# LayerNorm stage of a spectral-filter and GEGLU kernel: table loaded in pieces, row sums redistributed, last tiles grouped, transform waits per row tile

## The chip, the cores and the metric

The kernel runs on one core of a Trainium2 chip. The metric is device time in microseconds (us) of one execution. TensorE is called PE, VectorE DVE, ScalarE ACT, GpSimd POOL; SP issues most of the transfers (DMA).

## The reference

```python
h  = x + irfft2(rfft2(layernorm(x)) * (w_r + 1j*w_i))        # x: 2048 x 576, bf16
h2 = h + (gelu(layernorm(h) @ w_gate) * (layernorm(h) @ w_up)) @ w_down   # 576 -> 4608 -> 576
```

## The kernel before

The transforms are matmuls with cos/sin tables. Only the first stage matters here: the LayerNorm (LN1) of 16 row tiles of x and the first matmul, over the row index. Each tile of x (128 rows x 576) needs its mean and variance. The variance becomes 1/std, and that scales not x but the tile's slice of the cos/sin table `ATB`, giving `ATS`. The row-tile matmuls multiply x by `ATS` into PSUM; the results are evicted to `U`. When `U` is complete, the transform over the other index begins (`st_D`). Its first matmul is called **D** below.

```python
for i, (c0, c1) in enumerate(((0, 2), (2, 4), (4, 8), (8, 12), (12, 16))):
    P.dma(SP, XO[:, c0:c1, 0:D], xv[:, c0:c1, :], ...)           # x in five pieces
    if i == 1:
        P.dma(SP, ATB[...], dram["ATAB"][:, :], "atb", ...)      # whole table, 512 KB, after piece 2
...
GROUPS = ((0, 2), (2, 4), (4, 8), (8, 12), (12, 14), (14, 16))
ACT_TILES = (3, 7, 11, 13)            # sums of these tiles on ACT, the others on DVE (bn_stats)

ln1_act(3)                            # ACT: sum and sum of squares of tile 3
idle_mm(18)                           # 18 filler matmuls on a zero tile, to keep PE's clock up
ln1_tile(0); ln1_tile(1); ln1_var(0); ln1_sqrt(0)      # DVE, DVE, DVE, ACT
ln1_act(7)                            # ACT: needs x piece 3
ln1_tile(2); ln1_scale(0, DVE); ln1_var(1); ln1_sqrt(1); ln1_tile(4); ln1_scale(1, POOL)
a_group(0, (ACT,) * 5)                # row-tile matmuls of group 0 and their five evictions
# ... groups 1 to 5 in the same manner (cut) ...
idle_mm(2)

def st_D(i):                          # every d-transform matmul waits for all of U
    ... P.op(PE, matmul(bank, U[:, us, g, :, :], FT[:, o, dt, :]), r=ukeys + ["FT"], ...)
```

An instruction that waits holds what is written behind it on its engine.

## Time and profile before

| | before |
|---|---|
| time, median of the first 3 runs | 508.82 us |
| span of the profiled run | 506.9 us |
| D starts | 22.47 us |
| from D to the end | 484.4 us |

The page of the kernel before: busy time and share of the span by engine, then the chain of work that ended last, by line.

```profile
PE 496.6 (98%) x4331; PEld 290.1 (57%) x4331; DVE 182.4 (36%) x376; ACT 157.6 (31%) x296; POOL 46.1 (9%) x61
...
PE PS L740 56%; PE PS L761 28%; PE PS L634 2%; PE PS L649 2%; DMA XO<-in_A_x_dram 1%; PE PS L541 1%; PE PS L579 1%; DVE T_80 L563 1%; ACT U L476 1%; DVE CUS L547 1%; PE PS L558 1%; DVE CUS L548 1%; DVE T_81 L564 1%; DVE U L474 1%; ACT JNK L411 0%
```

L740 and L761 are the feed-forward matmuls, 84% of the chain. The LN1 stage is under 5% of the span, and everything after D is fixed work, so the change is worth what D moves forward. PE's 98% says little about this stage: of the first 22 us PE counts as busy for 16.96, and some 10 of them are fillers. The Trainium skill, "Trainium Kernel Development and Optimization" (section Performance Expectations), warns that matmul busy time is a poor metric; this trace agrees, since PE looks busy while D waits for DVE and ACT.

The timeline of PE in the kernel before (start us, duration us, engine, line, operation, count, and in brackets the idle time before it and its releaser):

```profile
1.32 6.12 PE L452 MATMUL PS<-ZD 128*128 128x512 bf16 x18 [1.32 <-POOL ZD L369]
7.74 0.96 PE L463 MATMUL PS<-ATS,XO 128*128 128x128 bf16 x10 [0.30 <-DVE ATS L447]
...
11.46 0.85 PE L463 MATMUL PS<-ATS,XO 128*128 128x128 bf16 x10 [2.44 <-POOL ATS L442]
...
22.47 1.66 PE L541 MATMUL PS<-FT,U 128*128 128x290 bf16 x12 [0.35 <-DVE U L474]
```

L452 are the fillers, L463 the row-tile matmuls, L541 is D. The first row-tile matmul is at 7.74 us.

The chain of waits of the kernel before, in order of time (start us, us, what):

```profile
2.13 6.73 DMA XO<-in_A_x_dram
8.88 0.78 ACT JNK L411 x2
...
10.32 0.18 ACT RS_56 L435
10.51 1.33 ACT U L476 x5
...
20.67 1.66 DVE U L474 x5
22.33 0.14 issue
22.47 0.55 PE PS L541 x3
```

The third x piece lands at 8.86 us. ACT's sums of tile 7 (`JNK`) wait for it, and behind them stand the second group's Sqrt (`RS_56`) and all evictions (`U`). From there ACT has no pause until its last eviction, and DVE waits for ACT only twice, for 0.84 and 0.36 us. So the chain starts with a transfer, and the 512 KB table had been queued in front of that transfer.

### The profile page before, as it was taken

What the parts mean: (1) busy time and instruction counts of PE and PEld (TensorE: products, weight loads), DVE (VectorE), ACT (ScalarE), POOL (GpSimd) and SP (SyncE); (2) the same over time, 40 slices, a digit from 0 to 9 for tenths busy, and PEclk for the clock granted to TensorE, in tenths of its full rate; (3) what the DMA queues carried; (4) which work ended last, traced back from release to release, by engine and by line L of the source; (5) the groups of instructions that cost most, each with busy time, mean ns of one, the idle gap of its engine ahead of it and who ended that gap; (6) DMA issues with size and microseconds to landing.
All of it is one profiled execution on the core that took longest, in us unless ns stands there. A gap on an engine that the chain in (4) does not pass through costs nothing.

```text
span 506.9 us, 9999 instructions
## 1 busy us (share of the span) xinstructions
PE 496.6 (98%) x4331; PEld 290.1 (57%) x4331; DVE 182.4 (36%) x376; ACT 157.6 (31%) x296; POOL 46.1 (9%) x61
## 2 busy tenths in 40 slices
PE   6899999999999999999999999999999999999997
PEld 2578675444447774444467744444577644444776
DVE  4899673335331114443311134433211233333111
ACT  5788776663230002333310023232200132323000
POOL 3278860000000000000000000000000000000000
PEclk9899999999999999999999999999999999999999
DMA  8679798001100000100000001100000000000000
GB/s 298 151 231 321 246 334 297 1 1 23 25 9 14 17 19 14 23 19 1 1 7 17 19 12 23 25 5 1 1 19 17 13 1 1 1 1 1 13 18 19
DMA packets 25660, 28.64 MB, mean 57 GB/s; under 512 B 11408, under 2 KB 19600, under 8 KB 25488
## 3 DMA queue, kind: packets, MB, share of 16 engines
q1 hardware_dynamic: 23040, 17.39, 11.9%
q0 software_dynamic: 2576, 10.62, 6.3%
q8 instruction: 34, 0.56, 0.5%
q14 instruction: 10, 0.08, 0.1%
HBM read 23.66 MB, written 2.36 MB: 51 GB/s over the span
## 4 chain that ended last, share of the span: by engine, by line
PE 90%; DVE 4%; ACT 2%; DMA 1%; issue 1%; POOL 0%; SPq 0%; DVEq 0%; POOLq 0%
PE PS L740 56%; PE PS L761 28%; PE PS L634 2%; PE PS L649 2%; DMA XO<-in_A_x_dram 1%; PE PS L541 1%; PE PS L579 1%; DVE T_80 L563 1%; ACT U L476 1%; DVE CUS L547 1%; PE PS L558 1%; DVE CUS L548 1%; DVE T_81 L564 1%; DVE U L474 1%; ACT JNK L411 0%
## 5 line engine op out<-in xcount | busy, mean ns | idle before, releaser
L752 ACT ACTIVATE GL<-PS 128x512 bf16<-128x512 f32 x144 | 85.9, 597 | 289.9 <-PE PS L740 289.9
L753 DVE TENSOR_TENSOR AT<-GL,PS 128x512 bf16<-128x512 bf16 x144 | 98.8, 687 | 174.3 <-PE PS L740 172.6
L740 PE MATMUL PS<-HT_69,WGU 64*128 64x512 bf16 x1296 | 144.4, 376 | 0.0
L740 PE MATMUL PS<-HT_84,WGU 64*128 64x512 bf16 x1296 | 144.4, 376 | 0.0
L761 PE MATMUL PS<-WD,AT 128*128 128x288 bf16 x1152 | 141.8, 286 | 0.0
L761 PEld LDWEIGHTS PS<-WD,AT 128*128 128x128 bf16 x1152 | 112.4, 98 | 29.9 <-issue 1.7
L740 PEld LDWEIGHTS PS<-HT_84,WGU 64*128 64x128 bf16 x1296 | 64.5, 94 | 77.9 <-issue 0.5
L740 PEld LDWEIGHTS PS<-HT_69,WGU 64*128 64x128 bf16 x1296 | 64.5, 94 | 76.8 <-issue 0.7
L764 DVE TENSOR_TENSOR OS<-PS,XO 128x288 bf16<-128x288 f32 x32 | 14.6, 457 | 126.0 <-PE PS L761 126.0
L652 DVE SCALAR_TENSOR_TENSOR XO<-PS,XO 128x576 bf16<-128x576 f32 x16 | 12.1, 756 | 11.3 <-PE PS L649 11.3
L541 PE MATMUL PS<-FT,U 128*128 128x290 bf16 x96 | 14.4, 287 | 0.4 <-DVE U L474 0.4
L634 PE MATMUL PS<-DT,V 128*128 128x289 bf16 x96 | 14.5, 287 | 0.2 <-DVE V L587 0.2
L579 PE MATMUL PS<-VT,ZS 128*128 128x256 bf16 x96 | 12.9, 272 | 0.4 <-POOL ZS L568 0.2
L585 ACT ACTIVATE V<-PS 128x768 bf16<-128x768 f32 x15 | 12.0, 810 | 1.1 <-PE PS L579 0.7
L558 PE MATMUL PS<-CUS,BT 128*128 128x289 bf16 (+2 forms) x96 | 10.7, 247 | 1.4 <-DVE CUS L548 1.0
L564 DVE TENSOR_TENSOR T_81<-YS,WS 128x580 bf16<-128x580 bf16 x16 | 11.9, 746 | 0.0
L636 ACT ACTIVATE GS<-PS 128x578 bf16<-128x578 f32 x16 | 10.3, 652 | 5.0 <-PE PS L634 4.9
L561 ACT ACTIVATE YS<-PS 128x578 bf16<-128x578 f32 x16 | 10.5, 654 | 4.5 <-PE PS L558 2.8
L568 POOL TENSOR_TENSOR ZS<-T_81 128x290 bf16<-128x290 bf16 x13 | 11.6, 894 | 1.9
L452 PE MATMUL PS<-ZD 128*128 128x512 bf16 x30 | 10.4, 501 | 1.3 <-POOL ZD L369 1.3
L418 DVE BATCH_NORM_STATS2 ST_53<-XO 128x6 f32<-128x288 bf16 x24 | 9.4, 442 | 4.4 <-DMA XO<-in_A_x_dram 4.4
L541 PEld LDWEIGHTS PS<-FT,U 128*128 128x128 bf16 x96 | 9.2, 98 | 2.9 <-issue 0.8
(61 smaller groups left out, 189.8 us busy)
## 6 DMA issues: line engine op xcount, KB each, us to landing
WD<-in_B_w_down_dram POOLq DMA_DIRECT2D x9, 576.0 KB, 19.7
WGU<-in_B_w_up_dram SPq DMA_DIRECT2D x4, 1152.0 KB, 12.5
WGU<-in_B_w_gate_dram POOLq DMA_DIRECT2D x4, 1152.0 KB, 10.1
out_dram<-OS SPq DMA_DIRECT2D x32, 72.0 KB, 1.6
XO<-in_A_x_dram SPq DMA_DIRECT2D x3, 576.0 KB, 7.7
IT<-c_itab SPq DMA_DIRECT2D x1, 1024.0 KB, 6.7
HT_84<-HN SPq DMA_TRANSPOSE x40, 2.4
XO<-in_A_x_dram SPq DMA_DIRECT2D x2, 288.0 KB, 3.1
```

The source lines that it names most:

```text
L541: P.op(PE, lambda t, b=b, o=o, dt=dt, us=us, g=g: t.matmul(bank(b, 0, 128, 0, 2 * HK), U[:, us, g, :, :], FT[:, o, dt, :], start=(dt == 0) ...
L558: P.op(PE, lambda t, b=b, tb=tb, pl=pl, q0=q0, q1=q1, m=m, sl=sl, sp_=sp_: t.matmul(bank(b, 0, 128, q0, q1), BT[:, sp_, tb, :], CUS[:, sl, ...
L564: P.op(DVE, lambda v, g=g, sl=sl: v.tensor_tensor(T2[:, sl, :, :], YS[:, sl, :, :], WS[:, g, 1::-1, :], op=ALU.mult), r=[("Y", sl)] + wk, ...
L579: P.op(PE, lambda t, b=b, o=o, c=c, zp=zp, sl=sl, sp_=sp_: t.matmul(bank(b, 0, 128, o, o + 256), ZS[:, sl, zp, 128 * c:128 * c + 128], VT[ ...
L585: P.op(ACT, lambda a, g=g, src=src: a.activation(V[:, :, :, g, :], src, ACTF.Copy), r=rk, w=[("V", g, 0)])
L634: P.op(PE, lambda t, b=b, h=h, i=i, kt=kt, c=c: t.matmul(bank(b, 0, 128, 0, K2), V[:, kt, c, :, :], DT[:, 3 * h + i, 0:K2], start=(i == 0) ...
L652: P.op(DVE, lambda v, x2=x2, c=c, sl=sl: v.scalar_tensor_tensor(x2, banks(4 + 2 * sl, 2, 288), 1.0, x2, op0=ALU.mult, op1=ALU.add, accum_o ...
L740: op = P.op(PE, lambda t, h0=h0, kt=kt, wt=wt, f=f, b=b, HT=HT, s=(half == 0 and j in (0, 5)), e=(half == 1 and j in (3, 8)): t.matmul(ban ...
L752: P.op(ACT, lambda a, s2=s2, b0=b0: a.activation(GL[:, s2, :], bank(b0), ACTF.Gelu_apprx_tanh), r=[("PS", b0)], w=[("GL", s2)])
L753: P.op(DVE, lambda v, s2=s2, b0=b0, f=f: v.tensor_tensor(AT[:, f, :], GL[:, s2, :], bank(b0 + 1), op=ALU.mult), r=[("GL", s2), ("PS", b0 + ...
L761: P.op(PE, lambda t, b=b, h=h, f=f, p=p: t.matmul(bank(b, 0, 128, 0, 288), AT[:, f, 128 * p:128 * p + 128], WD[:, f, 288 * h:288 * h + 288 ...
L764: P.op(DVE, lambda v, b=b, h=h, p=p, c=c: v.tensor_tensor(OS[:, p % 2, 288 * h:288 * h + 288], bank(b, 0, 128, 0, 288), XO[:, c, 288 * h:2 ...
```

## The change

Its intent is to get x pieces to the engines earlier and to cut the work on ACT and DVE before D: only 128 KB of table go in front of x piece 3; tile 1's sums go to ACT; the last four tiles form one group, so there is one Sqrt and five evictions fewer; each d-transform matmul waits only for the row tile of U that it reads. Cut to its core:

```diff
+    x_load(0, 0, 2)
+    x_load(1, 2, 4)
+    atb_load(0, 0, 4)
+    x_load(2, 4, 8)
+    atb_load(1, 4, 8)
+    x_load(3, 8, 12)
+    x_load(4, 12, 16)
+    atb_load(2, 8, 16)
-    GROUPS = ((0, 2), (2, 4), (4, 8), (8, 12), (12, 14), (14, 16))
-    ACT_TILES = (3, 7, 11, 13)
+    GROUPS = ((0, 2), (2, 4), (4, 8), (8, 12), (12, 16))
+    ACT_TILES = (1, 3, 7, 11, 13)
 ...
+    AORD = (0, 1, 4, 2, 3)            # row tiles in the order in which D needs them
     idle_mm(18)
+    act_sum(1); act_sq(1)
+    ln1_tile(0); ln1_tile(2); act_sum(3)
+    ln1_var(0); ln1_sqrt(0); act_sq(3)
+    ln1_rs(0); ln1_scale(0, DVE)
+    a_mms(0)
+    a_evs(0, ACT, (0,))               # first eviction ...
+    ln1_var(1)
+    ln1_sqrt(1)                       # ... stands in front of the second group's Sqrt on ACT
+    a_evs(0, ACT, (1, 2, 3, 4))
+    ln1_rs(1); ln1_scale(1, DVE)
+    idle_mm(2); a_mms(1)
+    ln1_tile(4); ln1_tile(5); ln1_tile(6)
+    act_sum(7); act_sq(7)
 ... (the rest of the order: 10, 5, 3 and 3 fillers before groups 2, 3, 4 and before D)
-                     r=ukeys + ["FT"], w=[("PS", b)])
+                     r=uk[us] + ["FT"], w=[("PS", b)])
```

More of the change, by code (lines that the diff above doesn't have):

```diff
@@ L373, in _build, with x_load, atb_load @@
     ov = out[0].rearrange("(p c) d -> p c d", c=NT)
-    for i, (c0, c1) in enumerate(((0, 2), (2, 4), (4, 8), (8, 12), (12, 16))):
+    tabs = dram["ATAB"].rearrange("p (c k) -> p c k", c=NT)
+    def x_load(i, c0, c1):
         P.dma(SP, XO[:, c0:c1, 0:D], xv[:, c0:c1, :], f"x{i}", w=[("X", c) for c in range(c0, c1)])
-        if i == 1:
-            P.dma(SP, ATB[:, :, :].rearrange("p a b -> p (a b)"), dram["ATAB"][:, :], "atb", w=["ATB"])
+    def atb_load(i, c0, c1):
+        P.dma(SP, ATB[:, c0:c1, :], tabs[:, c0:c1, :], f"atb{i}", w=[("ATB", c) for c in range(c0, c1)])
+    x_load(0, 0, 2)
[6 more added lines that the diff above has]
+    atb_load(2, 8, 16)
     P.dma(SP, FT[:, :, :, :].rearrange("p a b c -> p (a b c)"), dram["FTAB"][:, :], "ft", w=["FT"])
@@ L404, in _build, with act_sum, act_sq @@
     P.op(POOL, lambda g: g.memset(ZS[:, :, :, K2:ZW], 0.0), w=["Zz"])
-    GROUPS = ((0, 2), (2, 4), (4, 8), (8, 12), (12, 14), (14, 16))
-    ACT_TILES = (3, 7, 11, 13)
-    def ln1_act(c):
+    GROUPS = ((0, 2), (2, 4), (4, 8), (8, 12), (12, 16))
+    ACT_TILES = (1, 3, 7, 11, 13)
+    def act_sum(c):
         P.op(ACT, lambda a, c=c: a.activation(JNK[:, 0, :], XO[:, c, 0:D], ACTF.Identity, accum_out=SA[:, 0, c:c + 1]),
              r=[("X", c)], w=[("SA0", c), "J0"])
+    def act_sq(c):
         P.op(ACT, lambda a, c=c: a.activation(JNK[:, 1, :], XO[:, c, 0:D], ACTF.Square, accum_out=SA[:, 1, c:c + 1]),
@@ L436, in ln1_sqrt, with ln1_rs @@
              r=[("MV1", c) for c in range(c0, c1)] + ["EPT"], w=[("SD1", i)])
+    def ln1_rs(i):
+        c0, c1 = GROUPS[i]
+        P.op(DVE, lambda v, c0=c0, c1=c1: v.reciprocal(RS1[:, c0:c1], RS1[:, c0:c1]), r=[("SD1", i)], w=[("RS1", i)])
     def ln1_scale(i, eng):
         c0, c1 = GROUPS[i]
-        P.op(DVE, lambda v, c0=c0, c1=c1: v.reciprocal(RS1[:, c0:c1], RS1[:, c0:c1]), r=[("SD1", i)], w=[("RS1", i)])
         if eng == POOL:
@@ L443, in ln1_scale @@
                                                                RS1[:, c0:c1].unsqueeze(2).to_broadcast([128, c1 - c0, 128]), op=ALU.mult),
-                 r=[("RS1", i), "ATB"], w=[("ATS", c) for c in range(c0, c1)])
+                 r=[("RS1", i)] + [("ATB", c) for c in range(c0, c1)], w=[("ATS", c) for c in range(c0, c1)])
         else:
@@ L447, in ln1_scale @@
                 P.op(DVE, lambda v, c=c: v.tensor_scalar(ATS[:, c, :], ATB[:, c, :], RS1[:, c:c + 1], None, op0=ALU.mult),
-                     r=[("RS1", i), "ATB"], w=[("ATS", c)])
+                     r=[("RS1", i), ("ATB", c)], w=[("ATS", c)])
     def idle_mm(n):
@@ L476, in a_ev, with a_mms, a_evs @@
             P.op(ACT, lambda a, s=src, d=dst: a.activation(d, s, ACTF.Copy), r=[("PS", b)], w=[("U", i, k)])
-    def a_group(i, engs, between=None, at=5):
-        for k in range(5):
+    def a_mms(i):
+        for k in AORD:
             a_mm(i, k)
-            a_ev(i, k, engs[k])
-            if k == at:
-                between()
+    def a_evs(i, eng, ks):
+        for k in ks:
+            a_ev(i, AORD[k], eng)
+    AORD = (0, 1, 4, 2, 3)
     P.op(ACT, lambda a: a.activation(SA[:, 0, 0:1], EPT[:, 0:1], ACTF.Sqrt), r=["EPT"], w=[("SA0", 0)])
-    A5 = (ACT,) * 5
-    ln1_act(3)
     idle_mm(18)
+    act_sum(1)
+    act_sq(1)
     ln1_tile(0)
-    ln1_tile(1)
+    ln1_tile(2)
+    act_sum(3)
     ln1_var(0)
     ln1_sqrt(0)
-    ln1_act(7)
-    ln1_tile(2)
+    act_sq(3)
+    ln1_rs(0)
     ln1_scale(0, DVE)
+    a_mms(0)
+    a_evs(0, ACT, (0,))
     ln1_var(1)
     ln1_sqrt(1)
+    a_evs(0, ACT, (1, 2, 3, 4))
+    ln1_rs(1)
+    ln1_scale(1, DVE)
+    idle_mm(2)
+    a_mms(1)
     ln1_tile(4)
-    ln1_scale(1, POOL)
-    a_group(0, A5)
-    ln1_act(11)
     ln1_tile(5)
     ln1_tile(6)
+    act_sum(7)
+    act_sq(7)
+    a_evs(1, ACT, (0, 1))
     ln1_var(2)
     ln1_sqrt(2)
-    idle_mm(1)
-    a_group(1, A5)
-    ln1_act(13)
+    a_evs(1, ACT, (2, 3, 4))
     ln1_tile(8)
+    ln1_rs(2)
     ln1_scale(2, POOL)
+    idle_mm(10)
+    a_mms(2)
+    act_sum(11)
+    act_sq(11)
     ln1_tile(9)
@@ L513, in _build @@
     ln1_var(3)
+    a_evs(2, ACT, (0,))
     ln1_sqrt(3)
     ln1_tile(12)
-    ln1_var(4)
-    ln1_scale(3, POOL)
-    idle_mm(5)
-    a_group(2, A5, lambda: ln1_sqrt(4), 2)
-    ln1_tile(14)
-    ln1_scale(4, POOL)
-    ln1_tile(15)
-    ln1_var(5)
-    idle_mm(4)
-    a_group(3, (ACT, DVE, ACT, DVE, ACT), lambda: ln1_sqrt(5), 0)
-    ln1_scale(5, DVE)
-    a_group(4, (ACT, DVE, ACT, DVE, ACT))
-    a_group(5, (DVE, ACT, DVE, ACT, DVE))
-    idle_mm(2)
-    ukeys = [("U", i, k) for i in range(len(GROUPS)) for k in range(5)] + ["Uz"]
+    ln1_rs(3)
+    ln1_scale(3, POOL)
+    a_evs(2, ACT, (1,))
+    act_sum(13)
+    act_sq(13)
+    ln1_tile(14)
+    ln1_tile(15)
+    ln1_var(4)
+    a_evs(2, ACT, (2,))
+    a_evs(2, DVE, (4,))
+    ln1_sqrt(4)
+    ln1_rs(4)
+    ln1_scale(4, DVE)
+    a_evs(2, ACT, (3,))
+    idle_mm(5)
+    a_mms(3)
+    a_evs(3, ACT, (0,))
+    a_evs(3, DVE, (1,))
+    a_evs(3, ACT, (2,))
+    a_evs(3, DVE, (3,))
+    a_evs(3, ACT, (4,))
+    idle_mm(3)
+    a_mms(4)
+    a_evs(4, DVE, (0,))
+    a_evs(4, ACT, (1,))
+    a_evs(4, ACT, (2,))
+    a_evs(4, DVE, (3,))
+    a_evs(4, ACT, (4,))
+    idle_mm(3)
+    uk = [[("U", i, k) for i in range(len(GROUPS))] + ["Uz"] for k in range(5)]
+    ukeys = [k for ks in uk for k in ks]
     def st_D(i):
@@ L592, in idle_ft @@
             P.op(PE, lambda t, b=b: t.matmul(bank(b, 0, 128, 0, 2 * HK), FT[:, 0, 0, 0:128], FT[:, 0, 0, :], start=True, stop=True), r=["FT"], w=[("PS", b)])
-    P.alias(["ATB", "J0", "J1", "ZD"] + [("ATS", c) for c in range(NT)], ["Vfree"])
+    P.alias(["J0", "J1", "ZD"] + [(n_, c) for n_ in ("ATB", "ATS") for c in range(NT)], ["Vfree"])
     for i in range(NG + 3):
```

## The prediction

> **What bounds the kernel now.** The page gives a span of 506.9 us, PE 98% busy; 84% of the chain of waits is the FFN's matmuls (L740, L761), which the change does not touch. All it touches lies before the first d-transform matmul (L541), at 22.47 us in the timeline. From there to the end the same 484.4 us of work follow, so the gain is what that matmul moves forward.
>
> **What bounds those 22.5 us.** Chain and timeline by engine: x piece 3 lands at 8.86 us; ACT has stood still 2.7 us for it, the second group's Sqrt queued behind. From 8.88 ACT is busy without a break to 21.8, DVE nearly so to 22.3. The table lands at 7.43 and holds the first scaling 1.1 us.
>
> **What changes, costed from the trace.**
> - DMA: 384 KB of table leave the way of x piece 3. At 337 GB/s (windows, 5 to 10 us) that is an estimated 1.15 us: landing about 7.7; pieces 4 and 5 come 0.75 us earlier (10.3 and 11.7 now). Table piece 1 lands about 5.5. Two more issues (0.42 us each) delay the W loads under 1 us; they have over 2 to spare.
> - Tile 1 goes to ACT: -0.72 us DVE, +1.34 us ACT, mostly in ACT's idle time.
> - One group less: a Sqrt (0.19), a reciprocal (0.17) and five evictions fewer; ten 256-wide (ACT 0.27, DVE 0.34) become five 512-wide (0.48, 0.58): about 0.5 us.
> - Group 2's scaling moves from POOL to DVE (0.34); the last group's four tiles are on DVE (0.7).
>
> Walking the queues in order with these durations: the first scaling is ready at 6.3, but the 18 fillers in front end at 7.44, as before, so group 1's matmuls start at 7.44 (now 7.74), group 2 at 8.9 (11.46), group 3 at 13.5 (14.74), group 4 at 16.3 (17.98), the last at 19.5 (20.57). DVE becomes the limiting queue: it begins group 3's sums only at 8.9. In the last group matmuls end at 21.2, the last eviction at 21.8, three fillers (0.65 us) at 21.8. Waiting per row tile frees the d transform's first half from one or two last evictions (0.5 us), but the fillers hide most of that. L541 begins at about 21.7: gain 0.7 us, all critical, none given back later.
>
> **Clock.** The Trainium skill, "TensorE: Matmul & The Clock Gate" (Part 1: The HAM clock gate), says PE runs at half clock until about 3.4 us of sustained work. This trace agrees: fillers are 0.43 us apart to 5.5 us, about 0.2 after, and the windows show 0.74 in 10 to 15 us after the idle 9.0 to 11.5. Ten new fillers should keep that stretch nearer 1.0; its matmuls wait for ATS anyway, so this is worth little.
>
> **Prediction: 508.1 us**, 0.7 below 508.82; range 506.9 to 509.0. Faster by over 2%: 0.5%; within 2%: 99%; slower: 0.5%.
>
> **What would show the steps.** Right: x piece 3 before 8 us; ACT's wait for it gone; group 1's matmuls at 7.4 with no wait for ATS; group 2 about 9; L541 first at 21.3 to 22.1; L541 to the end unchanged within 0.3 us. Wrong: L541 above 22.3, or later stages lengthening.
>
> **What would make it wrong.** Slow-clock matmuls in group 3 or 4; group 4's third row tile waiting for the bank of group 3's fourth eviction (1 us in my walk); ACT-DVE handovers longer than read; the DVE-bound stretch at 38 to 53 us shifting its DVE/POOL overlap (T operations take 0.45 or 0.9 us there), up to 1 us either way.

## The result

The changed kernel took 508.19 us (median of 4 runs, 508.08 to 508.48) beside 508.70 us for the kernel before (4 runs, 508.56 to 509.06). The ratio is 0.999 with a 95% interval of 0.9972 to 1.0007: the same, and by these runs alone not clear of noise. In a later session, with five rounds, the same kernel took 507.84 against 509.01 us (ratio 0.9976, interval 0.9963 to 0.9988). The gain is real, and it was 0.5 us once and 1.2 us once; the experiments suggest why it is not one number.

The page of the changed kernel, the same two lines:

```profile
PE 497.0 (98%) x4340; PEld 290.5 (57%) x4342; DVE 182.5 (36%) x376; ACT 159.1 (31%) x296; POOL 44.8 (9%) x59
...
PE PS L787 56%; PE PS L808 28%; PE PS L681 2%; PE PS L696 2%; PE PS L469 1%; DVE ST_53 L432 1%; PE PS L626 1%; DVE T_80 L610 1%; PE PS L588 1%; DVE CUS L594 1%; PE PS L605 1%; DVE CUS L595 1%; DVE T_81 L611 1%; DVE U L491 0%; ACT YS L608 0%
```

The x transfer has left the chain, and a new entry stands there: PE L469, the fillers. The timeline of PE in the changed kernel (L469 fillers, L480 row-tile matmuls, L588 is D):

```profile
1.32 6.59 PE L469 MATMUL PS<-ZD 128*128 128x512 bf16 x18 [1.32 <-POOL ZD L369]
7.75 0.95 PE L480 MATMUL PS<-ATS,XO 128*128 128x128 bf16 x10
...
9.17 1.06 PE L480 MATMUL PS<-ATS,XO 128*128 128x128 bf16 x10
...
18.26 0.97 PE L480 MATMUL PS<-ATS,XO 128*64 128x128 bf16 x12 [0.83 <-ACT U L493]
...
21.89 1.66 PE L588 MATMUL PS<-FT,U 128*128 128x290 bf16 x12
```

D moved from 22.47 to 21.89, by 0.58 us. The span shrank by 0.5 (506.9 to 506.4), so from D to the end it is 484.5 us as before. Now the chain of waits of the changed kernel, in order of time:

```profile
1.32 6.59 PE PS L469 x18
8.06 0.38 ACT U L493
8.86 0.42 DVE ATS L464 x2
9.28 2.17 DVE ST_53 L432 x6
...
19.20 1.21 DVE U L491 x2
20.45 0.96 PE PS L480 x12
21.46 0.59 PE PS L469 x2
22.06 0.39 PE PS L588 x3
```

It no longer starts with a transfer. It starts with the 18 fillers. They end, the first row-tile matmuls follow at 7.75, ACT evicts the first at 8.06, behind that eviction stands the second group's Sqrt, behind the Sqrt DVE's scaling, and behind that DVE's sums of tiles 4 to 6. The waits of the changed kernel up to 30 us (engine, its line, what it waited for: us in total, times, longest) say the same:

```profile
DVE RS_56 L454 <- ACT RS_56 L449: 1.9, 2, 1.5
ACT U L493 <- PE PS L480: 1.8, 2, 1.3
```

x piece 3 lands at 7.83 us now (issued at 2.13, 5.7 us to landing), but DVE's first sum of tile 4 starts at 9.19: the data lie there for 1.36 us, longer than the 1.03 us by which they came earlier. The balance, with DVE's first sum of tile 4 as the mark:

| | starts tile 4 | D | stretch between |
|---|---|---|---|
| before | 8.88 | 22.47 | 13.59 |
| changed | 9.19 | 21.89 | 12.70 |

The stretch became 0.89 us shorter and its start 0.31 us later (1.05 us earlier by the transfer, 1.36 us later by the new wait): together the measured 0.58.

### The profile page after: what moved, and what is told of

Same layout as the page of the kernel before. It is cut to its first block, busy times and chain, and to the rows that moved or that the text cites. A ratio compares the mean times of both kernels' runs of the same rounds, so it can differ in the third digit from the quotient of the medians.

```text
span 506.4 us, 10019 instructions
## 1 busy us (share of the span) xinstructions
PE 497.0 (98%) x4340; PEld 290.5 (57%) x4342; DVE 182.5 (36%) x376; ACT 159.1 (31%) x296; POOL 44.8 (9%) x59
## 4 chain that ended last, share of the span: by engine, by line
PE 92%; DVE 6%; issue 1%; ACT 1%; POOL 0%; DVEq 0%; POOLq 0%
PE PS L787 56%; PE PS L808 28%; PE PS L681 2%; PE PS L696 2%; PE PS L469 1%; DVE ST_53 L432 1%; PE PS L626 1%; DVE T_80 L610 1%; PE PS L588 1%; DVE CUS L594 1%; PE PS L605 1%; DVE CUS L595 1%; DVE T_81 L611 1%; DVE U L491 0%; ACT YS L608 0%
## 5 line engine op out<-in xcount | busy, mean ns | idle before, releaser
L588 PE MATMUL PS<-FT,U 128*128 128x290 bf16 x96 | 14.4, 287 | 0.0
L469 PE MATMUL PS<-ZD 128*128 128x512 bf16 x39 | 11.9, 457 | 1.4 <-POOL ZD L369 1.3
L681 PEld LDWEIGHTS PS<-DT,V 128*128 128x128 bf16 x96 | 8.9, 97 | 3.4 <-issue 0.4
L696 PE MATMUL PS<-GS,IT 128*128 128x288 bf16 x64 | 10.5, 285 | 0.4 <-ACT GS L683 0.3
```

What stands on the lines that cost most here:

```text
L469: P.op(PE, lambda t: t.matmul(bank(7), ZD[:, 0:128], ZD[:, :], start=True, stop=True), r=["ZD"], w=[("PS", 7)])
L588: P.op(PE, lambda t, b=b, o=o, dt=dt, us=us, g=g: t.matmul(bank(b, 0, 128, 0, 2 * HK), U[:, us, g, :, :], FT[:, o, dt, :], start=(dt == 0) ...
L681: P.op(PE, lambda t, b=b, h=h, i=i, kt=kt, c=c: t.matmul(bank(b, 0, 128, 0, K2), V[:, kt, c, :, :], DT[:, 3 * h + i, 0:K2], start=(i == 0) ...
L696: P.op(PE, lambda t, b=b, h=h, i=i, c=c, rhs=rhs: t.matmul(bank(b, 0, 128, 0, 288), IT[:, h * i, c, :], rhs, start=(i == 0), stop=(i == 1) ...
```

## The experiments

Theory A: in the kernel before, the landing of x piece 3 is the gate; in the changed kernel the end of the fillers is. Theory B, the rival: the transfers and fillers are not what sets the stage; the queues of ACT and DVE are, and the gain comes from the new order and the fewer evictions. Every kernel below gave the right result. In the expectations groups are counted from 1, so "group 2" is the one that the code calls 1. All comparisons are of five timed rounds, the three groups of runs were on three chips, and "before" is the kernel before in the same session: 509.02 us in the first group of runs, 509.01 in the second, 508.88 in the third.

### The table in pieces, alone

```diff
 # kernel before
-    (x loads, whole table after piece 2)
+    x_load(0, 0, 2); x_load(1, 2, 4); atb_load(0, 0, 4); x_load(2, 4, 8); atb_load(1, 4, 8)
+    x_load(3, 8, 12); x_load(4, 12, 16); atb_load(2, 8, 16)
```

> The kernel before with the table load alone changed (three pieces, as in the change). Theory A (in the kernel before, the landing of x piece 3 holds ACT, and ACT is then busy without a break, so an earlier landing moves the whole stage): x piece 3 lands at about 7.8 us as in the changed kernel (8.86 before), ACT's sums of tile 7 start there, the first d-transform matmul comes at about 21.5 us (22.47 before), and the time is about 1.0 us below the kernel before, so about 0.5 us below the whole change. Theory B (the queues of ACT and DVE set the stage, not the transfers; the gain came from the new order and the fewer evictions): the first d-transform matmul stays within 0.3 us of 22.47 and the time is the same as before.

Measured: 507.98 us, 1.04 below the kernel before (ratio 0.9979, interval 0.9966 to 0.9993). The timeline of ACT in this kernel, the first sum of tile 7:

```profile
7.73 0.68 ACT L423 ACTIVATE JNK<-XO 128x576 bf16<-128x576 bf16 x1 [1.66 <-DMA XO<-in_A_x_dram]
```

and the timeline of PE, D (L553 here):

```profile
21.32 1.66 PE L553 MATMUL PS<-FT,U 128*128 128x290 bf16 x12 [0.35 <-DVE U L486]
```

D comes 13.59 us after the start of these sums, exactly as in the kernel before (22.47 - 8.88). Theory A holds for the kernel before. This one part of the change, alone, gains as much as the whole change did at its best. The Trainium skill, "DMA: Bandwidth & Descriptors" (section Queues, rings and completion order), says that descriptors on a ring are taken in order; this trace is in line with it: taking 384 KB away from in front of x piece 3 brought its landing forward from 8.86 to 7.73 us. The landing also varies by itself: over all traces it is 8.4 to 8.9 us with the whole table in front and 7.5 to 8.4 with 128 KB.

### The changed kernel with the table whole again

```diff
-    atb_load(0, 0, 4) ... atb_load(1, 4, 8) ... atb_load(2, 8, 16)
+    atb_load(0, 0, 16)                  # between x pieces 2 and 3, as before
```

> The changed kernel with the table loaded whole again, in its old place between x pieces 2 and 3. Theory A (in the changed kernel the fillers and the first eviction hold the second group's Sqrt until 8.3 us, so DVE reaches x piece 3 only at 9.2, later than its old landing at 8.86): table at 7.4, x piece 3 at 8.9, but the first d-transform matmul at 21.8 to 22.1 (21.89 in the changed kernel) and the time within 0.2 us of the changed kernel: the transfer order buys nothing here. Theory B (the gain is the transfer order): the first d-transform matmul falls back to about 22.4 or later, time 0.5 us up or more.

Measured: 508.0 us, 1.02 below the kernel before. The timeline of PE, the first row-tile matmuls (L478 here) and D (L586):

```profile
7.67 0.94 PE L478 MATMUL PS<-ATS,XO 128*128 128x128 bf16 x10
...
21.61 1.66 PE L586 MATMUL PS<-FT,U 128*128 128x290 bf16 x12
```

The changed kernel stood 0.51 and 1.17 us below the kernel before in its two sessions, so undoing the transfer order cost it nothing that can be seen. Theory A's odd consequence holds: the part that gained 1.0 us by itself buys nothing inside the changed kernel. The transfers came earlier than expected in this trace (the table at 7.0 us, x piece 3 at 8.4), but DVE reached tile 4 only at 9.11, again behind the fillers, the first eviction and the Sqrt. One small thing is unexplained: D follows the first row-tile matmul by 13.94 us here and by 14.14 in the changed kernel. The last group's scaling ran as four operations in 0.74 us here, and with a pause of 0.18 us after the first there; the other kernel with the whole table (below) has no such pause, but neither has the combined kernel, whose table comes in pieces. Why was not tested.

### All of U awaited again

```diff
-                     r=uk[us] + ["FT"], ...
+                     r=ukeys + ["FT"], ...
```

> The changed kernel with every d-transform matmul waiting for all U again, as before the change. Theory A: the last ACT eviction ends at 22.05 us, so the first d-transform matmul moves from 21.89 to about 22.15 and the time rises by 0.2 to 0.3 us; the wait per row tile is then worth about half of the change's 0.5 us. Theory B (fillers hide it all): no difference over 0.1 us.

Measured: 508.31 us, 0.71 below the kernel before. First row-tile matmul at 7.86, D at 22.26: 14.40 us after it, against 14.14 in the changed kernel. So the waits per row tile are worth 0.26 us by these traces (0.22 against the 14.18 of the second trace of the changed kernel, below), inside the 0.2 to 0.3 expected. The medians alone would not show it.

### The second group's Sqrt ahead of the first eviction

```diff
-    a_evs(0, ACT, (0,))
     ln1_var(1)
     ln1_sqrt(1)
-    a_evs(0, ACT, (1, 2, 3, 4))
+    a_evs(0, ACT, (0, 1, 2, 3, 4))
```

> The changed kernel with the second group's Sqrt ahead of the first eviction on ACT, nothing else. Theory A (that Sqrt waits 1.35 us behind an eviction that waits for PE's fillers, and DVE idles 1.5 us for it): Sqrt at about 7.15 us (8.34 now), DVE starts tile 4 at about 7.9 (9.19), ACT's sums of tile 7 then hold DVE some 0.6 us, so the first d-transform matmul comes 0.6 to 0.9 us earlier, at 21.0 to 21.3, and the time falls by as much. Theory B (DVE's idle time there is slack, taken up later by the bank wait of group 4 and the last fillers): first d-transform matmul within 0.2 us of 21.89.

Measured: 507.31 us, 1.71 below the kernel before (ratio 0.9967). The timelines of ACT (the Sqrt), of DVE (the sums from tile 4 on) and of PE (D):

```profile
7.24 0.30 ACT L449 ACTIVATE RS<-MV,EPT 128x2 f32<-128x2 f32 x1 [0.50 <-DVE MV L444]
```

```profile
8.10 2.25 DVE L432 BATCH_NORM_STATS2 ST<-XO 128x6 f32<-128x288 bf16 x6
```

```profile
20.81 1.66 PE L587 MATMUL PS<-FT,U 128*128 128x290 bf16 x12
```

D came even earlier than expected. The Sqrt waited for DVE's variances and not for PE, so DVE's start on tile 4 no longer hangs on the fillers. From that start to D it is 12.71 us, as in the changed kernel (12.70), so D's 1.08 us are DVE's earlier start (1.09). Not all of this is due to the Sqrt's place: the 18 fillers happened to end early here, with the first row-tile matmul at 6.89 instead of 7.75. The kernel with 14 fillers (below) has that matmul at 6.89 too, with the Sqrt behind the eviction, and there DVE starts tile 4 at 8.33 and D comes at 21.05. Beside that trace the Sqrt's place is worth some 0.24 us. What it is worth when the fillers end late is not shown: ACT's evictions and its sums of tile 7 still stand behind the first row-tile matmul.

### The changed kernel again

> The changed kernel unchanged, for the same rounds as the runs beside it. First d-transform matmul (called D below) 14.0 to 14.3 us after the first row-tile matmul, which follows the 18 fillers; these ended anywhere from 6.9 to 7.9 us in the five traces with this start, by when PE's clock rose. Time about 0.6 us below the kernel before.

Measured: 507.84 us, 1.17 below the kernel before. This trace has its first row-tile matmul at 7.00 and D at 21.18, 14.18 us later. So the same program has its fillers end at different times. PE runs them 0.43 us apart until its clock rises and 0.22 us apart after that, and the moment of the rise differs from run to run: between about 4.2 and 6.8 us in the traces. The Trainium skill, "TensorE: Matmul & The Clock Gate" (Part 1: The HAM clock gate), says that the activity window is free-running, so the number of slow matmuls varies from run to run; the traces agree, with a first row-tile matmul between 6.69 and 7.86 us after the same 18 fillers of the same order of work. In the two profiled runs of the changed kernel D moves with the first row-tile matmul. That the change was worth 0.5 us in one session and 1.2 in another for the same reason is an inference: the unprofiled runs have no trace, and chips and sessions may differ in other ways.

### 14 fillers, and 22

```diff
-    idle_mm(18)
+    idle_mm(14)      # and in another kernel 22
```

> The changed kernel with 14 instead of 18 fillers in front of the first row-tile matmul. Theory A (in the changed kernel the end of the fillers starts the chain: first eviction, Sqrt of group 2, DVE's sums): first row-tile matmul at 6.7 to 6.9 us (7.75 in the first trace of the changed kernel), D 14.0 us later at 20.7 to 21.0, time 0.4 to 0.9 us below the changed kernel. Theory B (fillers are harmless, the chain starts at x piece 3): no difference, D at 21.6 or later. If fewer fillers leave PE at half clock, the granted clock of 5 to 15 us falls well below 1.0 and D comes later than 21.9.

> The changed kernel with 22 instead of 18 fillers in front of the first row-tile matmul: four more at 0.215 us each, 0.86 us. Theory A (the end of these fillers starts the changed kernel's chain): first row-tile matmul at 7.7 to 8.7 us, D (the first d-transform matmul) 14.1 to 14.2 us after it, at 21.9 to 22.9; the time rises by 0.5 to 0.9 us over the changed kernel, back to within 0.5 us of the kernel before. Theory B (slack): no change.

Measured with 14: 507.21 us, 1.80 below the kernel before and 0.63 below the changed kernel of the same session; its five runs lie within 0.44 us, those of the changed kernel within 0.86. The timeline of PE with 14 fillers:

```profile
6.89 0.94 PE L480 MATMUL PS<-ATS,XO 128*128 128x128 bf16 x10
...
21.05 1.66 PE L588 MATMUL PS<-FT,U 128*128 128x290 bf16 x12
```

D is 14.16 us after the first row-tile matmul. The row-tile matmuls took as long as in the changed kernel (0.94, 1.06 and 1.52 us for the first three groups), so in this trace the four fillers were not needed for the clock. It was close: the fillers were still 0.43 us apart at 6.4 us. The column of the granted clock can't tell this, since it reads 1.00 from 0 us on, through the slow fillers too.

Measured with 22: 508.55 us beside 508.88, ratio 0.9999 (interval 0.9985 to 1.0012): no gain clear of noise is left of the change. The timeline of PE with 22 fillers:

```profile
1.32 6.87 PE L469 MATMUL PS<-ZD 128*128 128x512 bf16 x22 [1.32 <-POOL ZD L369]
8.03 0.95 PE L480 MATMUL PS<-ATS,XO 128*128 128x128 bf16 x10
...
22.17 1.66 PE L588 MATMUL PS<-FT,U 128*128 128x290 bf16 x12
```

D is again 14.14 us after the first row-tile matmul. In four traces of this order of work that distance is 14.14 to 14.18 us (and 12.70 to 12.73 from DVE's start of tile 4), while the start moves over 1.1 us and x piece 3 lands at 7.7 to 8.4 us. Theory A holds for the changed kernel, and Theory B, for which fillers were slack, falls.

### The kernel before with 22 fillers

```diff
 # kernel before
-    idle_mm(18)
+    idle_mm(22)
```

> The kernel before with 22 instead of 18 fillers. Theory A (there ACT waits for x piece 3 to 8.9 us and takes the first evictions only at 10.4, so the fillers have slack): first row-tile matmul up to 0.9 us later, D within 0.3 us of 22.47, time within 0.2 us of the kernel before. Theory B (fillers set the start in both kernels): D and time 0.5 to 0.9 us later.

Measured: 508.89 us beside 508.88. The timeline of PE:

```profile
7.85 0.84 PE L463 MATMUL PS<-ATS,XO 128*128 128x128 bf16 x10
...
22.27 1.66 PE L541 MATMUL PS<-FT,U 128*128 128x290 bf16 x12 [0.35 <-DVE U L474]
```

D is at 22.27, and ACT's sums of tile 7 start with the landing of x piece 3 at 8.69: 13.58 us between, as in the kernel before. PE's clock rose early in the profiled run, so the fillers ended at 8.02 there, only 0.58 later than in the first trace, and the first row-tile matmul came only 0.11 later. So the trace alone is a weak test, but the five timed runs (508.80 to 509.25) lie within those of the kernel before (508.54 to 509.44): the extra fillers cost nothing that can be seen. In the kernel before fillers were slack. The change itself put them on the chain.

### No fillers before D

```diff
     a_evs(4, ACT, (4,))
-    idle_mm(3)
```

> The changed kernel without the three fillers between the last row-tile matmul and D. Theory A (the fillers, not the evictions, hold D; they hide what the wait per row tile could give): D about 13.8 us after the first row-tile matmul instead of 14.1; its first three matmuls go ahead of the last ACT eviction, and D's first eviction comes 0.3 to 0.4 us earlier, time lower by as much. Theory B (the last evictions hold D's second half anyway): D's first eviction and the time within 0.1 us of the changed kernel.

Measured: 507.64 us, 0.20 below the changed kernel of the session, which is not clear of noise. First row-tile matmul at 6.69, D at 20.33, 13.64 later, and D's first eviction on ACT at 21.02, 14.33 us after the first row-tile matmul instead of 14.75 in the changed kernel beside it. So D's first eviction did come 0.4 us earlier. But DVE, which needs D's second half too, had to wait for that half, held by the last evictions of U. This is the timeline of DVE in this kernel:

```profile
21.71 0.46 DVE L593 TENSOR_TENSOR CUS<-ES,PS 128x290 bf16<-128x290 f32 x1 [0.71 <-PE PS L587]
```

The first matmul that follows from it came 15.99 us after the first row-tile matmul; in the changed kernel's two traces this is 16.14 and 16.17. Some 0.2 of the 0.4 us survived. Each theory was half right.

### Whole table and 14 fillers

```diff
 # changed kernel
-    atb_load(0, 0, 4) ... ; idle_mm(18)
+    atb_load(0, 0, 16);     idle_mm(14)
```

> The changed kernel with the table whole in its old place and 14 fillers. Theory A (fillers and transfers are two gates side by side; with 18 fillers the transfer order bought nothing, with 14 it does): the whole table (7.0 to 7.4 us) now holds the first row-tile matmul at 7.2 to 7.8 instead of 6.9, DVE starts tile 4 no earlier than x piece 3's landing at 8.4 to 8.9 instead of 8.3; D at 21.2 to 21.7 against 21.05, time 0.2 to 0.6 us above the changed kernel with 14 fillers. Theory B (the transfer order is worth nothing in this order of work): D within 0.1 us of 21.05.

Measured: 507.97 us, 0.91 below the kernel before, where 14 fillers with the table in pieces gave 1.80. The fillers end at 6.6 us, but the whole table lands at 7.4, so the first row-tile matmul comes at 7.69 and D at 21.75. With fewer fillers the transfer order matters again, by some 0.7 us in the traces. Both are more than expected: D is 0.05 us past the range, and the time is 0.89 us above that kernel (each taken against the kernel before of its session) instead of 0.2 to 0.6. Fillers and table are two gates at the same door: with 18 fillers moving the table shows nothing, and with the whole table removing fillers shows little.

### Both gates off the chain

```diff
 # changed kernel
     a_mms(0)
-    a_evs(0, ACT, (0,))
     ln1_var(1); ln1_sqrt(1)
-    a_evs(0, ACT, (1, 2, 3, 4))
+    act_sum(7); act_sq(7)
+    a_evs(0, ACT, (0, 1, 2, 3, 4))
-    ln1_rs(1); ln1_scale(1, DVE)
+    ln1_rs(1); ln1_scale(1, POOL)
     ... sums of tiles 11 and 13 likewise ahead of the evictions of groups 1 and 2,
     ... Sqrt of groups 2, 3 and 4 right after their variances,
-    idle_mm(10)   # before group 2
+    idle_mm(6)
-    idle_mm(3)    # before D
```

> The changed kernel with: group 2's Sqrt and ACT's sums of tiles 7, 11 and 13 ahead of the evictions that they had stood behind, group 2's scaling back on POOL, all but one of group 3's evictions on ACT, 6 instead of 10 fillers before group 3, none before D. Theory A (queue order on ACT, then DVE's own work, set the stage): DVE starts tile 4 at the landing of x piece 3, about 7.8 us, whenever the fillers end; D at 19.9 to 20.5 us; time 1.3 to 1.9 us below the changed kernel. Theory B (something else holds the last group): D not below 20.8, as with the Sqrt alone moved.

Measured: 506.74 us, 2.27 below the kernel before (ratio 0.9954, interval 0.9942 to 0.9967) and 1.10 below the changed kernel of the same session. It beats both. Its timelines of ACT and of PE:

```profile
7.62 0.68 ACT L423 ACTIVATE JNK<-XO 128x576 bf16<-128x576 bf16 x1 [0.19 <-DMA XO<-in_A_x_dram]
```

```profile
7.12 0.95 PE L480 MATMUL PS<-ATS,XO 128*128 128x128 bf16 x10
...
19.48 2.08 PE L585 MATMUL PS<-FT,U 128*128 128x290 bf16 x12
```

ACT takes tile 7 the moment its data lands, and D is at 19.48, earlier than the 19.9 to 20.5 expected. Part of that is not fully paid out: with no fillers D's second half waits, as above. The first matmul after D's results came at 21.89, against 23.17 in the changed kernel of the session. That is 1.28 us, and the time fell by 1.10, less than the 1.3 to 1.9 expected.

Then 22 fillers in it:

```diff
 # combined kernel
-    idle_mm(18)
+    idle_mm(22)
```

> The combined kernel with 22 instead of 18 fillers. Theory A (Sqrt and sums no longer stand behind evictions, so the fillers are off the chain): DVE starts tile 4 at 7.6 to 7.9 us still; ACT's first eviction, at 9.0, waits at most 0.4 us for PE; D within 0.4 us of 19.48 and the time within 0.3 us of the combined kernel. Theory B: 0.5 to 0.9 us later, as in the changed kernel.

Measured: 506.27 us, 2.61 below the kernel before (ratio 0.9948). The first row-tile matmul moved from 7.12 to 8.76 us and D did not move: 19.45. This is the timeline of PE:

```profile
8.76 0.95 PE L480 MATMUL PS<-ATS,XO 128*128 128x128 bf16 x10
...
19.45 2.08 PE L585 MATMUL PS<-FT,U 128*128 128x290 bf16 x12
```

Here 1.64 us of delay cost D nothing; in the changed kernel 0.3 us of it showed in D in full. So the fillers no longer set D, but the slack is about used up: ACT's first eviction, at 9.07, follows the first row-tile matmuls directly here, and the chain of this trace starts with the fillers. It was 0.47 us below the combined kernel in medians, 0.34 after taking off the difference of the sessions, a little over the 0.3 expected and in the direction no theory called for; the two intervals overlap, and it is not read as a gain.

## Why the prediction was right or wrong

- **The time: right.** 508.1 was predicted and 508.19 measured, then 507.84; both lie in the range of 506.9 to 509.0. D was expected at about 21.7; it was at 21.89 and 21.18. That 508.19 came so close to 508.1 is partly luck: in the second trace the fillers ended 0.75 us earlier, and D came 0.71 us earlier with them.
- **What bounded the kernel before: right.** D stays 13.58 to 13.59 us behind ACT's sums of tile 7, which start with the landing of x piece 3, in three traces with three starts (8.88, 8.69, 7.73).
- **The walk through the queues: right in order, 0.2 to 0.5 us too early.** Predicted starts of the groups 7.44, 8.9, 13.5, 16.3, 19.5; measured 7.75, 9.17, 14.03, 16.80, 19.71. The predicted wait for the bank of the fourth eviction is there with 0.83 us (predicted 1). "DVE begins group 3's sums only at 8.9" was the step that mattered, and it was at 9.19.
- **"The 18 fillers in front end at 7.44, as before": the step that was mis-stated.** The end of the fillers was treated as a constant. It is the start of the changed kernel's chain, and it wandered: 18 fillers let the first row-tile matmul start anywhere from 6.69 to 7.86 us. So the predicted gain of 0.7 was the middle of a spread, not a size.
- **x pieces 4 and 5 "come 0.75 us earlier": wrong, without effect.** They landed at 10.2 and 11.7 us (3.08 + 7.1 and 3.55 + 8.1), against 10.3 and 11.7, and DVE took their first tiles only at 11.90 and 14.67. Piece 3 was right: 7.83 for 7.7.
- **Waiting per row tile, "the fillers hide most of that": partly right.** It is worth 0.26 us; without the last fillers some 0.2 us more.
- **New fillers for the clock, "worth little": not shown.** No run took them out alone. The windows of 10 to 15 us show 0.74 before and 1.00 after; the table in pieces alone also showed 1.00 there, without the new fillers. So they were not needed for the clock there. The clock's rise at the start came 4.2 us after the first filler in the kernel before (1.32 to about 5.55), and 2.9 to 5.5 us after it over all traces, not at 3.4. The two lines of the windows are given below.
- **What the prediction did not see:** that one part, the table in pieces, would gain 1.0 us alone, and that the rest of the change, which shortens the stretch before D by 0.89 us, would hold DVE behind Sqrt, eviction and fillers until 1.36 us after the landing, so that the two gains do not add up.

The windows of 10 to 15 us: busy time by engine, then the granted clock, DMA share and GB/s. First the kernel before:

```profile
10.00:15.00 5.00, 3.28 (x18) 1.42 (x19) 4.37 (x18) 5.00 (x19) 1.65 (x2) 0.74 1.08 338
```

and the changed kernel:

```profile
10.00:15.00 5.00, 3.15 (x27) 1.73 (x27) 4.79 (x23) 4.52 (x16) 1.04 (x1) 1.00 1.07 354
```

## What to carry to other kernels

When a change moves a gate, look at what stands next in each in-order queue: here a transfer left the chain and the fillers, harmless until then, took its place by way of one eviction written in front of a Sqrt. Filler matmuls are instructions in front of real work, and their end moves with the clock's rise, so nothing that another engine needs should hang on the first result behind them. And when a change has several parts, run each alone: the best part of this one was worth as much as the whole.

## What the Trainium skill lacked or had wrong

- "TensorE: Matmul & The Clock Gate" (Part 1) rightly says that the number of slow matmuls varies from run to run, and calls the ramp under 1% of a typical span. It does not say that fillers put in for the ramp carry that variation into the work behind them: the first useful matmul came at 6.69 to 7.86 us after the same 18 fillers, a spread of 1.17 us, as much as the whole change was worth at its best.
- The same page (section Why this matters for your kernels) advises against idle gaps over about 3 us. In two traces shorter gaps went before a slow clock: after 2.44 us (kernel before, granted clock 0.50 from 13 to 15 us) and 2.25 us (kernel before with 22 fillers, 0.50 from 12 to 15 us) the following fillers ran 0.43 us apart. After gaps of 1.39 and 1.85 us the clock stayed at 1.00. No run varied the gap alone.
- No page gives the price of ACT's accumulated sums. A pass of 128x576 lasted 0.67 to 0.68 us and the read of the accumulator behind it 0.19 us, but the two overlap: in the traces the read starts 0.57 to 0.59 us after the pass and the next pass 0.09 to 0.10 us after the read, so both together take 0.67 us of ACT.
